# Loads of u, v and z kept apart from DMA block turns, outputs moved to the turns' queue, a third output buffer

## The chip, the cores and the metric

The kernel runs on one core of a Trainium2 chip. The metric is the device time of one execution in microseconds (us). Before the change three runs took 961.69, 960.47 and 951.78 us, median 960.47 us. A further execution was profiled; it took 950.05 us, and its span from first to last instruction is 948.3 us.

The engines' short names are those of the profile: PE (TensorE, matrix products), DVE (VectorE), ACT (ScalarE), POOL (GpSimd) and SP (SyncE). POOL and SP issue the DMA transfers here, each in the order of its own instruction stream; an instruction that waits holds back all that stands behind it in that stream.

## The reference

For each of 8 batches of 3072 rows, `u` and `v` have 256 columns, `z` has 64:

```python
scores = (1.0 / S) * np.matmul(z, z.transpose(0, 2, 1))
attn = np.maximum(scores, 0.0) ** 2
x = u * np.matmul(attn, v)                      # attention with a gate
g = np.maximum(x @ w1, x @ w2)                  # 1024 columns
out = g @ w_out                                 # 24576 x 256, float32
```

The scores of a batch are symmetric, so a block of `attn` right of the diagonal is also, transposed, a block left of it.

## The kernel before

**Tiles.** Rows come in tiles of 128 (24 in a batch), groups of 4 tiles (`G`, 6 in a batch), and couples of 2 groups (3 in a batch, named (b, c)). `attn` is kept in blocks of 4 x 4 tiles, `blk`, 128 partitions x 2048 bf16, 512 KB each; 27 slots (`NSLOTS`) are used in turn.

**Scores.** `score_pair` (line 190) makes two tiles' worth of a block: two matmuls from `zT` into PSUM (`s_ps`, four buffers), Relu by ACT into `r_sb` (line 217), the square by DVE into the block (lines 223, 225). Only blocks on and right of the diagonal are computed. A block right of the diagonal is turned by one DMA transpose into the slot of its mirror image (`mirror`, line 244, issued on SP). A diagonal block is computed as a triangle from batch 1 on, and three small DMA transposes fill the rest (line 228). A turn may be issued once its scores are there and its target slot is free.

**The first four groups** (batch 0, groups 0 to 3) run in a plain form (lines 619 to 699), with products at line 262. Some of their mirrors wait in the list `later` and are turned during groups 1 to 3.

**A couple** (loop at line 747, products at line 835). From batch 1 on, the product of a couple with `v` is made by seven products of half size in place of eight. Their operands are sums of blocks (S1, S3 ahead, S2, S4 during the couple; `combine`, line 297, DVE at line 300) and of pieces of `v` (`combine_v`, line 157: four differences, in the tile `vt`). Each product is worked by the two halves of PE's rows, at different times, in two lanes (`LANES`); where the halves of one product follow each other, the second waits for a `nop` on POOL that waits for the first (the relay, lines 844 to 849). The sums stand in four PSUM banks, `acc0` to `acc3`. Score pairs of later blocks are spread evenly over the couple's steps, so the turns come out evenly too, and the last scores of a couple are finished just after its last step.

**After a couple's last step** comes, in program order:

1. `loads_behind(i)` (line 704): loads of `u` for the next couple, and of pieces of `v` and `z` for the next batch, all issued on POOL;
2. DVE's work for the next couple: S1 and S3 of three block groups, at the first couple of a batch with `combine_v` of three pieces of `v` ahead of them (the first two differences of the piece loaded last stand fifth and sixth), and then the gates (line 415), which multiply by the turned `u` (`uT`);
3. `ff(i-1)` on PE (line 426): the gated unit and the output product of the couple before. It puts its four sums into the same banks `acc0` to `acc3` (`banks`, line 430). `leave` (line 471) copies each to SBUF on ACT (`o_sb`, line 475) and sends it to HBM (line 476): two half-way, two at the end.

Then the next couple begins. Its steps 2 and 6 issue the turns of `u` (`turn_u`, line 178, two buffers, freed by the gates of the couple before), step 8 or 30 the turn of a piece of `z` (`turn_z`, line 130), and then come the block turns. The recording is done under a manual schedule: each engine's instructions stand in the order in which they are written, and semaphores are set from the tiles that they read and write.

**Queues.** SP issues all turns (`mirror`, the triangles, `turn_u`, `turn_z`), and the four outputs of the last couple. POOL issues all loads and the other 92 outputs. A tile pool with n buffers lets its (n+1)th tile wait for the release of the first: `opool` has 2 buffers, so the third output copy waits until the first output has landed.

The names to follow: `load_z` 122, `turn_z` 130, `load_v` 142, `combine_v` 157, `load_u` 174, `turn_u` 178, `mirror` 244, `ff`/`leave` 426/471, `loads_behind` 704.

## Time and profile before

| What | Value |
|---|---|
| Runs | 951.78 to 961.69 us, median 960.47 |
| Profiled execution | 950.05 us, span 948.3 us |
| Busy time of DVE, ACT, POOL | 683.5, 633.6, 140.4 us |
| Mean granted PE clock | 0.984 |
| DMA packets | 146.01 MB, mean 154 GB/s |
| Read from HBM, written | 59.77 MB, 25.17 MB |
| Mirrors and triangle turns (`blk<-blk`) | 246, 4.7 us from issue to landing |
| Output on POOL (`out_dram<-o_sb`) | 92, 256 KB each, 4.2 us to landing |
| Output on SP | 4, 256 KB each, 2.1 us to landing |
| Load of `v` / `u` / `z` (most) | 84 / 48 / 21; 128 / 256 / 128 KB in SBUF; 8.4 / 7.2 / 8.4 us to landing |

How to read it. Busy time is a union of the times of an engine's instructions; a PE that is busy is not at its peak. A line of waits reads: the engine and what it waited to do, what released it, us in total, number of times, longest. A line of a timeline reads: start and duration in us, engine, line, operation, output and input tile, number of instructions, and in brackets the idle time before it and what ended it; `SPq` is SP's sequencer, and the time of a DMA there is the time that its issue took. The time from issue to landing counts from the start of the issue until the semaphore of the transfer has risen.

### The profile page before, as it was taken

The page shows a single profiled execution, that of the slowest core. Times are in us where ns is not written, and L with a number is a line of the kernel's source. Part 1 is how long each engine was busy: PE and PEld are TensorE (multiplying, and loading weights), DVE is VectorE, ACT ScalarE, POOL GpSimd, SP SyncE. Part 2 cuts the span into 40 slices and gives each one's busy share as a digit, 9 for nine tenths or more (in the row PEclk, how much of TensorE's full clock was granted, in tenths as well). Part 3 has the DMA queues.
Part 4 walks back from the last instruction along what each step waited for, and adds up shares of the span by engine and source line. Part 5 has one row for each costly group of instructions (what it writes and reads, how often), then busy time and mean ns, then how long its engine had stood idle before and what let it go on. Part 6 is the DMA issues. An engine that isn't in the chain of part 4 may idle for free.

```text
span 948.3 us, 19578 instructions
## 1 busy us (share of the span) xinstructions
PE 909.4 (96%) x7490; PEld 532.4 (56%) x7538; DVE 683.5 (72%) x1043; ACT 633.6 (67%) x1219; POOL 140.4 (15%) x266
## 2 busy tenths in 40 slices
PE   9994799999999999999989999999979999999998
PEld 4453355675655655655546656566445664655655
DVE  6770369696897689786786968968768687795542
ACT  6783587667676777767756677776746767674443
POOL 3121022020210210220202102102111021101000
PEclk9998799999999999999999999999999999999999
DMA  9999796999988988989989899799996987996401
GB/s 183 167 190 149 151 214 121 195 119 199 187 128 182 178 155 160 176 139 190 141 145 194 129 175 176 132 207 133 172 148 126 193 160 150 160 116 134 96 18 73
DMA packets 391838, 146.01 MB, mean 154 GB/s; under 512 B 362944, under 2 KB 377664, under 8 KB 391744
## 3 DMA queue, kind: packets, MB, share of 16 engines
q1 hardware_dynamic: 359904, 91.14, 61.9%
q0 software_dynamic: 31840, 53.62, 29.5%
q8 instruction: 59, 0.97, 0.4%
q14 instruction: 35, 0.29, 0.1%
HBM read 59.77 MB, written 25.17 MB: 90 GB/s over the span
## 4 chain that ended last, share of the span: by engine, by line
PE 85%; issue 4%; DMA 4%; SPq 2%; DVE 2%; POOL 1%; ACT 1%; ACTq 0%; DVEq 0%; POOLq 0%
PE acc L835 41%; PE acc L457 19%; PE d_ps L435 15%; PE s_ps L204 6%; PE acc L262 4%; DMA out_dram<-o_sb 3%; SPq L246 2%; DMA blk<-blk 1%; POOL v_sb L150 0%; DVE blk L300 0%; ACT r_sb L217 0%; DVE blk L225 0%; PE acc L597 0%; DVE blk L223 0%; ACT o_sb L475 0%
## 5 line engine op out<-in xcount | busy, mean ns | idle before, releaser
L217 ACT ACTIVATE r_sb<-s_ps 128x512 bf16<-128x512 f32 (+3 forms) x664 | 331.1, 559 | 113.4 <-PE s_ps L204 72.6
L835 PE MATMUL acc<-blk,vt 64*128 64x512 bf16 x2016 | 370.8, 379 | 9.9 <-ACT o_sb L475 9.9
L835 PE MATMUL acc<-blk,v_sb 64*128 64x512 bf16 x1704 | 345.8, 380 | 18.2 <-DMA blk<-blk 18.0
L300 DVE TENSOR_TENSOR blk<-blk,blk 128x2048 bf16<-128x2048 bf16 x252 | 302.0, 1221 | 23.2 <-PE acc L835 17.9
L448 ACT ACTIVATE g_sb<-d_ps 128x512 bf16<-128x512 f32 x376 | 217.9, 602 | 110.6 <-PE d_ps L435 89.9
L225 DVE TENSOR_TENSOR blk<-r_sb 128x1024 bf16<-128x1024 bf16 x251 | 170.5, 691 | 141.1 <-ACT r_sb L217 138.9
L457 PE MATMUL acc<-w_out_sb,g_sb 128*128 128x256 bf16 x1536 | 226.5, 273 | 0.0
L435 PE MATMUL d_ps<-xT,w_sb 128*128 128x512 bf16 x720 | 214.2, 379 | 2.6 <-issue 0.2
L835 PEld LDWEIGHTS <-vt 64*128 64x128 bf16 x2016 | 154.1, 95 | 92.8 <-issue 8.1
L835 PEld LDWEIGHTS <-v_sb 64*128 64x128 bf16 x1704 | 133.6, 95 | 119.0 <-DMA blk<-blk 18.3
L457 PEld LDWEIGHTS <-g_sb 128*128 128x128 bf16 x1536 | 150.3, 98 | 83.9
L204 PE MATMUL s_ps<-zT 64*128 64x512 bf16 (+3 forms) x672 | 148.6, 360 | 0.9 <-DVE r_sb L215 0.5
L476 POOL DMA_DIRECT2D out_dram<-o_sb x92 | 49.9, 547 | 381.8 <-ACT o_sb L475 366.9
L475 ACT COPY o_sb<-acc 128x512 f32<-128x512 f32 x96 | 52.1, 590 | 62.3 <-DMA out_dram<-o_sb 34.1
L435 PEld LDWEIGHTS <-w_sb 128*128 128x128 bf16 x768 | 73.3, 98 | 28.2 <-issue 9.8
L223 DVE TENSOR_TENSOR blk<-r_sb 128x512 bf16<-128x512 bf16 (+3 forms) x170 | 46.4, 320 | 40.0 <-ACT r_sb L217 39.8
L204 PEld LDWEIGHTS <-zT 64*128 64x128 bf16 x672 | 45.8, 95 | 47.9 <-issue 13.0
L150 POOL DMA_DIRECT2D v_sb<-in_v_dram x90 | 48.5, 566 | 148.3 <-PE acc L835 107.1
L771 DVE TENSOR_TENSOR h_sb<-h_sb,acc 128x512 f32<-128x512 f32 x84 | 55.4, 681 | 6.7 <-PE acc L835 6.7
L415 DVE SCALAR_TENSOR_TENSOR xT<-h_sb,uT 128x512 bf16<-128x512 f32 x96 | 59.9, 684 | 0.0
L176 POOL DMA_DIRECT2D un<-in_u_dram x48 | 26.2, 559 | 207.7 <-PE acc L835 161.5
L262 PE MATMUL acc<-blk,v_sb 64*128 64x512 bf16 x384 | 50.8, 376 | 1.7 <-DVE blk L225 1.1
(50 smaller groups left out, 274.8 us busy)
## 6 DMA issues: line engine op xcount, KB each, us to landing
out_dram<-o_sb POOLq DMA_DIRECT2D x92, 256.0 KB, 4.2
un<-in_u_dram POOLq DMA_DIRECT2D x48, 256.0 KB, 7.2
v_sb<-in_v_dram POOLq DMA_DIRECT2D x84, 128.0 KB, 8.4
blk<-blk SPq DMA_TRANSPOSE x246, 4.7
zn<-in_z_dram POOLq DMA_DIRECT2D x21, 128.0 KB, 8.4
v_sb<-in_v_dram POOLq DMA_DIRECT2D x6, 256.0 KB, 7.5
blk<-in_moe_w_dram POOLq DMA_DIRECT2D x2, 512.0 KB, 7.0
out_dram<-o_sb SPq DMA_DIRECT2D x4, 256.0 KB, 2.1
```

The source lines that it names most:

```text
L204: nc.tensor.matmul(s_ps[h][:, lo[h] :], zT[rows, z_at(b, blk * G + tiles[h]), :], zT[rows, q + lo[h] // P : q + G, :].rearrange("p t c -> ...
L217: nc.scalar.activation(o, s, AF.Relu)
L225: nc.vector.tensor_mul(a[:, k : k + 2, :], r, r)
L262: nc.tensor.matmul(a.out(acc[half, dc]), v_at(b, t, dc)[rows], a.moving(rows, j), start=first, stop=last,)
L300: op(*((by_key(x) if mixed else x.ap) for x in blocks))
L415: lambda dc=dc: nc.vector.scalar_tensor_tensor(out=x[:, dc, :].rearrange("p (t r) -> p t r", r=P), in0=hs[dc].rearrange("p (t r) -> p t r" ...
L435: nc.tensor.matmul(d_ps, w15_sb[:, kc, ts(nb, P)], xs[q][:, kc, :], start=(kc == 0), stop=(kc == KD - 1),)
L448: nc.scalar.activation(g_sb[q, nb], d_ps, AF.Relu)
L457: nc.tensor.matmul(o_ps[key][:, t % 2, :], x[:, ts(t, P)], w, start=first, stop=ends and t % 2 == 1 and n == len(weights) - 1,)
L475: nc.scalar.copy(o_sb, o_ps[q, h])
L771: nc.vector.tensor_add(out, a, b_)
L835: mm = nc.tensor.matmul(a.out(acc[name]), w()[rows], a.moving(rows, j), start=first, stop=left[name] == 0, skip_group_check=True,)
```

## The change

Four edits go together. (1) Two helpers, `turn` and `load`, wrap the DMA calls. A load marked `alone` waits until the last turn that was issued before it, in program order, has landed; the next turn or output behind a group of such loads waits until the last load of the group has landed. Only the first of several loads, and the first of several turns or outputs, carries the wait. All loads of `loads_behind` are marked so. (2) All outputs are issued on SP. (3) `opool` has three buffers. For that room, `vt` shrinks from four parts to three: the difference B22 - B12 overwrites B12 in the loaded piece of `v`, and P7 reads its weights there. (4) Two early loads in batch 0 (`z` piece 2 and `v` piece 2 of batch 1), which began during group 3 behind a small memset each, move into `loads_behind` of couple (0, 1), with `load_v(1, 1)`.

```diff
-    opool = ctx.enter_context(tc.tile_pool(name="opool", bufs=2))
+    opool = ctx.enter_context(tc.tile_pool(name="opool", bufs=3))
...
+    turned, loaded = [], []
+
+    def behind(go, others):
+        while others:
+            tc.add_manual_dep(go.ins, others.pop().ins.name, AFTER, reason="one at a time")
+
+    def turn(out, in_):
+        go = nc.sync.dma_start_transpose(out, in_)
+        behind(go, loaded)
+        turned[:] = [go]
+
+    def load(out, in_, alone=False):
+        go = nc.gpsimd.dma_start(out=out, in_=in_)
+        if alone:
+            behind(go, turned)
+            loaded[:] = [go]
...
-        nc.sync.dma_start_transpose(
+        turn(
...
-        t = tpool.tile([P, 4, G, P], bf16, name="vt")
+        t = tpool.tile([P, 3, G, P], bf16, name="vt")
...
-            lambda: nc.vector.tensor_sub(t[:, 2], b22, b12),
+            lambda: nc.vector.tensor_sub(b12, b22, b12),
             lambda: nc.vector.tensor_sub(t[:, 1], b22, t[:, 0]),
-            lambda: nc.vector.tensor_sub(t[:, 3], b21, t[:, 1]),
+            lambda: nc.vector.tensor_sub(t[:, 2], b21, t[:, 1]),
...
-        "P7": ("S3", 2),
+        "P7": ("S3", 12),
...
-        "X21": ("A22", 3),
+        "X21": ("A22", 2),
...
                 nc.scalar.copy(o_sb, o_ps[q, h])
-                (nc.sync if last else nc.gpsimd).dma_start(out=dst, in_=o_sb)
+                behind(nc.sync.dma_start(out=dst, in_=o_sb), loaded)
...
-                if (i, n) == (3, 14):
-                    load_z(1, 2, held=True)
-                if (i, n) == (3, 18):
-                    load_v(1, 2, held=True)
...
         def loads_behind(i):
             b, c = couples[i]
+            if (b, c) == (0, 1):
+                load_z(1, 2, alone=True)
             if c == 2 and b + 1 < B:
-                load_v(b + 1, 0)
+                load_v(b + 1, 0, alone=True)
             if i + 1 < len(couples):
                 for q in range(2):
-                    load_u(couples[i + 1][0], 2 * couples[i + 1][1] + q)
+                    load_u(couples[i + 1][0], 2 * couples[i + 1][1] + q, alone=True)
+            if (b, c) == (0, 1):
+                load_v(1, 2, alone=True)
+                load_v(1, 1, alone=True)
             if b and b + 1 < B and c < 2:
-                load_z(b + 1, c + 1)
-                load_v(b + 1, c + 1)
+                load_z(b + 1, c + 1, alone=True)
+                load_v(b + 1, c + 1, alone=True)
             if c == 2 and b + 2 < B:
-                load_z(b + 2, 0)
+                load_z(b + 2, 0, alone=True)
...
         loads_behind(PLAIN // 2 - 1)
-        load_v(1, 1)
```

More of the change, by code (lines that the diff above doesn't have):

```diff
@@ L120, in zT_pe, with load_z @@
         copy(zT[:, lo : lo + n, :], tp)
-    def load_z(b, piece, held=False):
+    def load_z(b, piece, held=False, alone=False):
         zn[b, piece] = zpool.tile([P, 2 * G, dqk], bf16, name="zn")
@@ L125, in load_z @@
             nc.vector.memset(zn[b, piece][:, 0, 0:1], 0.0)
-        nc.gpsimd.dma_start(
-            out=zn[b, piece], in_=by_tile(z[b])[:, ds(piece * 2 * G, 2 * G), :]
-        )
+        load(zn[b, piece], by_tile(z[b])[:, ds(piece * 2 * G, 2 * G), :], alone)
     def turn_z(b, piece):
@@ L140, with load_v @@
     vp, vt = {}, {}
-    def load_v(b, piece, lo=0, n=2 * G, held=False):
+    def load_v(b, piece, lo=0, n=2 * G, alone=False):
         if (b, piece) not in vp:
@@ L145, in load_v @@
         t = vp[b, piece]
-        if held:
-            nc.vector.memset(t[:, lo, 0:1], 0.0)
         step = 2 if b else n
         for at in range(lo, lo + n, step):
-            nc.gpsimd.dma_start(
-                out=t[:, ds(at, step), :], in_=by_tile(v[b])[:, ds(piece * 2 * G + at, step), :]
-            )
+            load(t[:, ds(at, step), :], by_tile(v[b])[:, ds(piece * 2 * G + at, step), :], alone)
     def v_at(b, t, dc):
@@ L164, in combine_v, with load_u @@
             lambda: nc.vector.tensor_sub(t[:, 0], b12, b11),
-            lambda: nc.vector.tensor_sub(t[:, 2], b22, b12),
+            lambda: nc.vector.tensor_sub(b12, b22, b12),
             lambda: nc.vector.tensor_sub(t[:, 1], b22, t[:, 0]),
-            lambda: nc.vector.tensor_sub(t[:, 3], b21, t[:, 1]),
+            lambda: nc.vector.tensor_sub(t[:, 2], b21, t[:, 1]),
         ]
     un, uT = {}, {}
-    def load_u(b, g):
+    def load_u(b, g, alone=False):
         un[b, g] = unat.tile([P, G, D], bf16, name="un")
-        nc.gpsimd.dma_start(out=un[b, g], in_=by_tile(u[b])[:, ds(g * G, G), :])
+        load(un[b, g], by_tile(u[b])[:, ds(g * G, G), :], alone)
     def turn_u(b, g):
         t = upool.tile([P, G, KD, P], bf16, name="uT")
-        nc.sync.dma_start_transpose(
+        turn(
             t.rearrange("p a c r -> p (a c) r"), un[b, g].rearrange("p a d -> p (a d)")
@@ L227, in finish @@
                 for j in range(G - 1):
-                    nc.sync.dma_start_transpose(
+                    turn(
                         a[:, j + 1 :, ts(j, P)], a[:, j, (j + 1) * P :]
@@ L245, in mirror @@
         t = Block(turned=True)
-        nc.sync.dma_start_transpose(
-            t.ap.rearrange("p (k r) -> p k r", r=P), A[b, g, blk].ap
-        )
+        turn(t.ap.rearrange("p (k r) -> p k r", r=P), A[b, g, blk].ap)
         A[b, blk, g] = t
```

## The prediction

> **What bounds the kernel now.** I read the busy shares first, then the waits of TensorE (PE), then the chain of waits inside one stall, and last the two DMA-issuing queues as a timeline.

> The page: PE is busy nearly everywhere, and so are the DMA engines, two thirds of that with block turns (q1), one third with loads and outputs (q0).

> ```profile
> PE 909.4 (96%) x7490; PEld 532.4 (56%) x7538; DVE 683.5 (72%) x1043; ACT 633.6 (67%) x1219; POOL 140.4 (15%) x266
> ...
> DMA  9999796999988988989989899799996987996401
> ...
> q1 hardware_dynamic: 359904, 91.14, 61.9%
> q0 software_dynamic: 31840, 53.62, 29.5%
> ```

> PE's idle time is 948.3 - 909.4 = 38.9 us, so no more can be won. The waits name its two large parts (us, times, longest), and one of SyncE's (SP's) that matters below:

> ```profile
> PE acc L835 <- DMA blk<-blk: 18.0, 1, 18.0
> PE acc L835 <- ACT o_sb L475: 9.9, 3, 5.7
> SPq L180 <- DVE xT L415: 61.6, 11, 10.4
> ```

> The chain of waits around the longest of the three `o_sb` stalls (start, us) shows its mechanism: an output lands, ScalarE (ACT) may overwrite that buffer, and only then has PE its bank back.

> ```profile
> 696.47 12.73 DMA out_dram<-o_sb
> ...
> 709.29 0.59 ACT o_sb L475
> ...
> 709.93 0.58 PE acc L835
> ```

> The granted clock, by stretch, tells the rest of a stall's price: it was 0.50 from 96 to 101 us, during the 18.0 us stall, and 0.71 from 710 to 716, after the 5.7 us one. A 6 us stretch at 0.71 loses 1.7 us; the 1.2 us stall has no such mark.

> Last the queues. SP behind the end of couple (1,2), T0 = 237.3 us, and GpSimd (POOL) at that end:

> ```profile
> 237.29 2.15 POOL L150 DMA_DIRECT2D v_sb<-in_v_dram  x4 [17.83 <-PE acc L835]
> 239.38 1.11 POOL L176 DMA_DIRECT2D un<-in_u_dram  x2
> 240.42 0.60 POOL L126 DMA_DIRECT2D zn<-in_z_dram  x1
> ```

> ```profile
> 256.99 2.66 SPq L180 DMA_TRANSPOSE uT<-un  x2
> 259.75 2.09 SPq L246 DMA_TRANSPOSE blk<-blk  x1
> 261.95 4.30 SPq L228 DMA_TRANSPOSE blk<-blk  x3
> 266.34 1.26 SPq L134 DMA_TRANSPOSE zT<-zd  x1
> 267.70 3.77 SPq L228 DMA_TRANSPOSE blk<-blk  x3
> 271.57 19.07 SPq L246 DMA_TRANSPOSE blk<-blk  x4
> ```

> SP works without a break from 257.0 on and still has four mirrors to issue when couple (2,0) ends at T0 = 272.2. They take 19 us because the loads run beside them. Alone, mirrors start 2.43 us apart (116.27, 118.78, 121.21, 123.60) and land 4.7 us after issue (page).

> **The change, part by part.** Let T0 be the end of a couple's steps. From the traces of PE, ACT and DVE behind 237.3: `ff` fills PE until T0+17.5 (254.81); the third and fourth `o_sb` copies come at T0+17.4 and 18.0; P5 needs the fourth copy's bank at T0+20.9 (258.2), and the third score pair, at T0+20.8 (258.06), needs ACT to have done the first.

> *Edits at nothing.* `vt` in three parts: `L165` takes 0.42 us wherever it writes, and weight loads from `vt` and `v_sb` both cost 95 ns; were the strided write twice as long, 0.4 us on DVE per piece. Two memsets go: POOL waits less, before anything needs it. 92 outputs leave POOL (0.54 us each) for SP, where four rows show 0.34 us: 1.4 us of SP per couple, in front of the `uT` turns; counted below.

> *Third buffer.* Now only the fourth copy waits for the first output's landing. This alone removes the three stalls: 9.9 us, and 1.7 us of slow clock behind the two larger ones, **-13.3 us**.

> *The wait of the loads.* They start when the last turn emitted has landed, not at T0. Seven loads (1.1 MB in SBUF): the last is issued 3.1 us after the first (240.42 - 237.29), and the least crowded z load landed in 3.4 us: at least 6.5. With bandwidth: at the start of the kernel 256 KB loads land 1.28 us apart (v issued 2.46, landing 6.4 later; the sixth after it issued 5.64, landing 10.9 later), so 4.5 x 1.28 plus 2.9 for the first bytes (3.6 us for the v load at 127.0, less its own 0.64) = 8.7 at most. I take D = 7.6.

> What stands behind the first waiting load on POOL: the other loads, and then the next couple's relay `nop`s (line 844), through which one half of PE's work waits for the other. P1 ends in lane 0 at T0+20.7 and its other half starts six steps of 0.22 us later, at T0+22.1. With the last turn at T0+14.1 (below) the loads are issued by T0+17.8: covered, by some 3 us; a turn that lands later than that makes PE wait for the relay.

> *The wait of the outputs.* The next item in SP's queue after the loads is the first output, so it waits for their landing, LL; behind it stand three outputs, two `uT` and the whole next train. Output lands 2.3 us later (2.1 on the page from SP), copy 0.6, two relus 1.1: PE's stall is S = LL + 4.0 - 20.8, that is **S = (LL - T0) - 16.8**. The other end counts P5's bank alone: S = (LL - T0) - 18.0.

> Now the three kinds of boundary.

> Behind c=2. The last mirrors wait for their scores, in before too: 346.55 is issued 1.3 us before T0 = 347.8, and two follow. Alone: 346.55 + 2 x 2.43 + 4.7 = T0+8.3; I take 7.5, since SP may be ahead. The fourth v load lands 5.3 us later, T0+12.8 (it was 8.4), and LL = T0+15.1: no output stall. But `combine_v` of this piece stands first on DVE, with 10 us of `vt` and `blk` work behind it: it ended at 255.7, and PE takes the last S3 at 258.5, so slack 2.8. Stall 12.8 - 8.4 - 2.8 = 1.6 (1.3 to 3.4). The gates behind move by 4.4, and SP's `uT` waits for them (the third line of waits): from T0+19.7 to 24.1.

> Behind c=0. The train from 256.99 to its landing, alone, is 271.57 + 3 x 2.43 + 4.7 - 256.99 = 26.6. So the last turn lands 24.1 + 26.6 = 50.7 after the old T0; the couple ends at 34.95 + 1.6 = 36.55: T0+14.1. LL = T0+21.7, **S = 4.9**, plus 1.7 of clock.

> Behind c=1. `uT` follow the fourth output, LL + 3.4 from the previous boundary; two uT, zT, three mirrors and twelve triangle turns at 1.28 land 28.9 later. The couple ends 36.5 + 6.6 after the previous T0. With LL = 21.7: 21.7 + 3.4 + 28.9 - 43.1 = T0+10.9, LL = T0+18.5, **S = 1.7**, and half of the clock's 1.7.

> Sum: batches 1 to 6, 6 x (6.6 + 2.6) = 55; seven boundaries behind c=2, 7 x 1.6 = 11; batch 7 loads only u, none. **+66 us.**

> *The stall at 83 us.* It ends with a mirror that loads held up (two mirrors issued at 66.27 and 71.12 took until 86.2). Alone, six more turns are issued by 77.3 and land at 82. But now eleven loads (10.5 us) follow, to 92.5, then `turn_z`, then the outputs: 96.2, copy, PE starts at 97 and not 101. The slow clock starts as early and then covers more work: I take **-2**; if turns and loads were both gone from this place, -18 - 2.5.

> From the profiled 950.05 us (span 948.3): 950.05 - 13.3 + 66 - 2 = **1000**. The profiled execution lies at the low end of the runs (median 960.47); I add nothing, because part of that spread may be the very `o_sb` stalls that go. With the cheap ends (D = 6.5, bank alone) S is 2.6 and about 0.6, sum +38: 973; with the dear ones (D = 8.7, c=2 stall 3.4) +90: 1025.

> [...]

> **The rivals.**
> 1. *The turns are done in time, and the kernel is faster* (12%). If LL comes by T0+16.8 behind c=0 and c=1, no output is late. For it: without loads beside them the trains end earlier than before, and source-bound turns may not queue up. Against it: SP is already unbroken from `uT` to the couple's end, and it starts no earlier. Price: 950.05 - 13.3 - 2 = 935, or 917 if the first stall goes too.
> 2. *A draw* (7%): output stalls of about 1 us at twelve boundaries and 0.5 us at seven, +15, cancel the gain: 950 to 970 with the runs' spread. A difference of 1% is about what this kernel's measurement can tell.
> 3. *Late turns hold up more than outputs* (8%). Turns 5 us later reach the S sums (`L300`; it waits for turns only 3.0 us now) and scores that reuse blocks, or the loads are issued after T0+20.7 and PE waits for POOL's relays. 2 us more at 20 boundaries: 1040.
> 4. The forecast (73%): 973 to 1025.

> Slower by over 1%: 81%. The range 956 to 1030 leaves out most of rivals 1 and 3.

> **What would show it.** Right: PE waits for `ACT o_sb` some 12 times or more, 2 to 6 us each, behind c=0 and c=1; POOL's loads wait for `DMA blk<-blk`; SP's output waits for a load; mirrors never take over 3 us to issue; the clock row dips all through. Wrong: PE's idle time below 30 us, or loads that land within 5 us of their first issue.

## The result, and the profile after

The changed kernel took 1062.70 us, median of 4 runs (1061.53 to 1069.21); the kernel before took 956.12 us beside it (4 runs, 951.24 to 961.69). The ratio is 1.113, 95% interval 1.104 to 1.122: slower by 11%. The prediction said slower, with 1000 us and a range up to 1030, so the direction held and the size did not: from the profiled 950.05 us it added 50, and the profiled execution after (1069.21 us, span 1067.3 us) adds 119. Some executions of a kernel are over 1.5% longer than its fastest; the medians here include them and the ratios do not, so a ratio need not be the quotient of two medians.

The page of the changed kernel, the busy shares, clock, DMA and queue lines that were shown of the kernel before:

```profile
PE 957.7 (90%) x7490; PEld 552.9 (52%) x7538; DVE 682.0 (64%) x1041; ACT 632.4 (59%) x1219; POOL 90.6 (8%) x174
...
PEclk9996989898999998989999989898899998999999
DMA  9998867868677696766968678686786867858212
...
q1 hardware_dynamic: 373152, 115.26, 54.9%
q0 software_dynamic: 24480, 29.50, 18.3%
```

The loss is in two parts. PE's idle time is 1067.3 - 957.7 = 109.6 us, up by 70.7. PE's busy time rose by 957.7 - 909.4 = 48.3 us for the same 7490 matmuls: the clock row now dips all through, and the mean granted clock fell from 0.984 to 0.942. The DMA row, 9 nearly everywhere before, is now mostly 6 to 8.

What the change was for did happen: 17 of the 246 block turns took over 3 us to issue, the longest 9.2, where 66 had before, the longest 15.0. The prediction's sign said that none would.

The waits of the changed kernel (us in total, times, longest):

```profile
POOL un L76 <- DMA blk<-blk: 207.7, 5, 43.6
...
PE acc L844 <- ACT o_sb L484: 62.0, 13, 19.3
DVE vt L175 <- DMA v_sb<-in_v_dram: 56.7, 7, 9.2
...
PE acc L844 <- DVE blk L309: 26.3, 17, 3.2
```

The stalls on output copies grew from 9.9 us in 3 to 62.0 us in 13: the six couple ends behind c=0, the six behind c=1, and the first couple's stall of 19.3 us, which before was put down to a mirror and lasted 18.0. The seven waits of DVE for `v`, and PE's for the S sums (`blk L309`), are the ends behind c=2. POOL's loads wait for turns and the clock dips, as written under what would show the prediction right.

The chain of waits behind couple (1,1) of the changed kernel (start, us) shows one output stall from end to end. The last turn had landed at 228.59.

```profile
229.14 0.86 POOL un L76 x2
...
232.26 6.70 DMA v_sb<-in_v_dram
238.96 0.02 SPq L485
...
239.01 2.02 DMA out_dram<-o_sb
...
241.13 0.59 ACT o_sb L484
...
241.76 0.61 PE acc L844 x2
```

The seventh load lands 9.8 us after the first was issued (238.96 - 229.14), within 0.05 us SP issues the first output, 2.0 us later it has landed, and only then may the fourth copy take its buffer. PE stood idle from 237.47 to 241.76. It is exactly the predicted chain; its first link is longer than was allowed for.

Then the clock, by stretch around that stall (us, PE busy and matmuls, the other engines, granted clock, DMA share, GB/s):

```profile
237.50:241.10 3.60, 0.00 (x0) 0.00 (x0) 0.00 (x0) 0.00 (x0) 0.00 (x0) 1.00 0.39 136
241.10:248.00 6.90, 6.24 (x29) 2.44 (x30) 2.75 (x6) 4.62 (x9) 0.00 (x0) 0.51 0.91 211
248.00:251.00 3.00, 3.00 (x32) 1.50 (x29) 3.00 (x4) 2.26 (x5) 0.00 (x0) 1.00 0.86 162
```

The 4.29 us of waiting are followed by 6.9 us at half clock: 29 matmuls in 6.24 us, where the next 3 us hold 32. That is another 3.1 us (6.24 x 0.49), or 3.5 us if it is reckoned by matmuls (6.24 - 29 x 3.0 / 32). Over the whole trace PE was busy for 91.8 us at half clock, before for 11.9 (busy time inside the stretches that the traces record at half clock). Half of the difference is 40 us, so slow clock accounts for most of the 48.3 us.

How the couples' stretches changed, each from the first product of `ff` behind its last step to the same point of the next couple (us, summed from the two traces):

| Stretch | Before | After | Difference | Predicted |
|---|---|---|---|---|
| first (0,1) | 61.4 | 63.6 | +2.2 | -2 |
| six behind c=0 | 218.8 | 249.1 | +30.4 | +39.6 |
| six behind c=1 | 223.4 | 269.6 | +46.2 | +15.3 |
| seven behind c=2 | 272.9 | 313.6 | +40.7 | +11.2 - 13.3 |

The three stalls of before lie in the last row, so the gain of the third buffer is counted there.

### The profile page after: what moved, and what is told of

Same layout as the page of the kernel before. It is cut to its first block, busy times and chain, and to the rows that moved or that the text cites. A ratio compares the mean times of both kernels' runs of the same rounds, so it can differ in the third digit from the quotient of the medians.

```text
span 1067.3 us, 19596 instructions
## 1 busy us (share of the span) xinstructions
PE 957.7 (90%) x7490; PEld 552.9 (52%) x7538; DVE 682.0 (64%) x1041; ACT 632.4 (59%) x1219; POOL 90.6 (8%) x174
## 2 busy tenths in 40 slices
DMA packets 397727, 146.01 MB, mean 137 GB/s; under 512 B 362945, under 2 KB 377665, under 8 KB 397633
## 3 DMA queue, kind: packets, MB, share of 16 engines
q1 hardware_dynamic: 373152, 115.26, 54.9%
q0 software_dynamic: 24480, 29.50, 18.3%
## 4 chain that ended last, share of the span: by engine, by line
PE 57%; DMA 20%; DVE 11%; issue 5%; POOL 4%; ACT 2%; SPq 0%; ACTq 0%; DVEq 0%; POOLq 0%
PE acc L844 31%; DMA v_sb<-in_v_dram 10%; PE acc L466 9%; PE d_ps L444 9%; DVE blk L309 6%; PE s_ps L215 5%; DMA blk<-blk 4%; DMA out_dram<-o_sb 3%; PE acc L271 3%; POOL v_sb L76 3%; DMA zn<-in_z_dram 1%; DVE blk L236 1%; DMA un<-in_u_dram 1%; POOL un L76 1%; DVE xT L424 1%
## 5 line engine op out<-in xcount | busy, mean ns | idle before, releaser
L844 PE MATMUL acc<-blk,v_sb 64*128 64x512 bf16 x2208 | 437.7, 398 | 54.0 <-DVE blk L309 26.3
L228 ACT ACTIVATE r_sb<-s_ps 128x512 bf16<-128x512 f32 (+3 forms) x664 | 329.8, 562 | 147.4 <-PE s_ps L215 64.9
L844 PE MATMUL acc<-blk,vt 64*128 64x512 bf16 x1512 | 346.9, 403 | 42.6 <-ACT o_sb L484 42.6
L309 DVE TENSOR_TENSOR blk<-blk,blk 128x2048 bf16<-128x2048 bf16 x252 | 301.6, 1219 | 33.8 <-PE acc L844 31.5
L844 PEld LDWEIGHTS <-v_sb 64*128 64x128 bf16 x2208 | 169.8, 98 | 224.1 <-issue 106.9
L215 PE MATMUL s_ps<-zT 64*128 64x512 bf16 (+3 forms) x672 | 187.1, 376 | 2.0 <-DVE r_sb L226 0.5
L844 PEld LDWEIGHTS <-vt 64*128 64x128 bf16 x1512 | 132.3, 99 | 91.1 <-issue 25.2
L215 PEld LDWEIGHTS <-zT 64*128 64x128 bf16 x672 | 58.7, 98 | 42.1 <-issue 11.2
L76 POOL DMA_DIRECT2D v_sb<-in_v_dram x90 | 48.3, 567 | 274.9 <-PE d_ps L444 194.2
L271 PE MATMUL acc<-blk,v_sb 64*128 64x512 bf16 x384 | 50.4, 376 | 2.3 <-DVE blk L236 1.1
L466 PE MATMUL acc<-W2o_sb,xT 128*128 128x256 bf16 x384 | 49.9, 273 | 0.7 <-DVE h_sb L290 0.7
```

Source lines behind the costliest of these rows:

```text
L76: go = nc.gpsimd.dma_start(out=out, in_=in_)
L215: nc.tensor.matmul(s_ps[h][:, lo[h] :], zT[rows, z_at(b, blk * G + tiles[h]), :], zT[rows, q + lo[h] // P : q + G, :].rearrange("p t c -> ...
L228: nc.scalar.activation(o, s, AF.Relu)
L271: nc.tensor.matmul(a.out(acc[half, dc]), v_at(b, t, dc)[rows], a.moving(rows, j), start=first, stop=last,)
L309: op(*((by_key(x) if mixed else x.ap) for x in blocks))
L466: nc.tensor.matmul(o_ps[key][:, t % 2, :], x[:, ts(t, P)], w, start=first, stop=ends and t % 2 == 1 and n == len(weights) - 1,)
```

## The experiments

The theory after the result: every wait of the change makes its own chain late, by the loads' landing and by the last turn's, and the chains hide each other; at each couple end the latest shows. The rivals: moving the outputs to SP's queue costs it (no wait needed), or whatever waits, the time in which loads have the DMA engines to themselves is lost.

The first six kernels take away the waits, or what makes a late output cost, in steps. All are the changed kernel with the edit shown.

**Outputs free of the loads**

```diff
-                behind(nc.sync.dma_start(out=dst, in_=o_sb), loaded)
+                nc.sync.dma_start(out=dst, in_=o_sb)
```

> The changed kernel, but no output waits for loads (loads still wait for the last turn, and the next turn for the loads). My theory: behind c=0 and c=1 PE stalls because the fourth output copy waits for the first output, and that one for the loads; these stalls (7 and 5 us long with their slow clock, some 75 us in all) go, those behind c=2, where VectorE waits for v, stay: 985 to 1000 us, and PE waits for the output copies under 10 us in all. Rival, the move of the outputs to SP's queue is what costs, because they stand behind turns there: 1050 us or more.

Measured: 1034.79 us, neither number. Behind c=0 the stalls are gone wholly (36.4 us a stretch, as in the kernel before). Behind c=2 the late `v` stays. Behind c=1 a new stall of 4.7 to 8.0 us begins 27 us after the couple's end. Its wait, and the chain at the one that ends at 241.87:

```profile
PE s_ps L215 <- DMA zT<-zd: 38.7, 6, 8.0
```

```profile
224.94 7.37 DMA zn<-in_z_dram
...
238.58 3.25 DMA zT<-zd
241.87 0.61 PE s_ps L215
```

This is a chain that the prediction's sum did not have: the next batch's `z` is loaded behind c=1, turned by `turn_z`, and needed by its first scores in the same couple. The load waits for the last turn, and then the turn of `z`, behind the two of `u`, waits for the last load. In the changed kernel, where no such wait shows, the output stall comes earlier in the couple and pushes these scores back.

**The `v` loads of c=2 at once**

```diff
-                load_v(b + 1, 0, alone=True)
+                load_v(b + 1, 0)
```

> The changed kernel, but the four loads of v behind c=2 do not wait for the last turn (u and z still do). My theory: the stalls behind c=2 come from the fourth v load, which now lands 15 to 17 us after the couple's end and has 10 us of VectorE work behind it; landing 7 to 9 us after the end it costs nothing, and 40 to 55 us of 55 go: 1005 to 1025 us. Rival, the outputs' wait is the cause behind c=2 as well: 1050 us or more.

Measured: 1039.79 us, 23 us less than the changed kernel and 15 more than the upper end of the expectation. The fourth `v` load now lands 6.4 to 7.0 us after the first product of `ff` behind a c=2 end (13.5 to 15.7 before this edit) and PE no longer waits for S sums. But the `u` and `z` loads still wait, and the output stalls, now 20, take the place:

```profile
PE acc L844 <- ACT o_sb L484: 82.7, 20, 17.7
```

**A fourth output buffer**, all waits kept (the room is taken from the gate products)

```diff
-    gpool = ctx.enter_context(tc.tile_pool(name="gpool", bufs=8))
-    opool = ctx.enter_context(tc.tile_pool(name="opool", bufs=3))
+    gpool = ctx.enter_context(tc.tile_pool(name="gpool", bufs=7))
+    opool = ctx.enter_context(tc.tile_pool(name="opool", bufs=4))
```

> The changed kernel with a fourth output buffer (and one of the eight buffers of the gate products given up to make room); all waits stay. Theory (behind the first and second couples PE waits because the fourth output copy needs the buffer of the first output, whose transfer is held until the loads have landed): no PE stall on output copies behind the first and second couples of the iterations, the v stall behind the third couples as in the changed kernel, the z turn stall of 4.7 to 8.0 us behind the second couples as where outputs are free; the time is within 10 us of 1034.8, the kernel with outputs that do not wait. Rival (the held outputs also crowd the turns behind them, buffers or not): 1050 us or more.

Measured: 1036.35 us, 1.6 us from the kernel with free outputs. The outputs are as late as in the changed kernel (issued 17 to 20 us after the first product of `ff` at c=0 ends), yet no fourth copy waits for one: behind c=0, where a stretch takes 36.4 us again, buffer reuse was the whole price of late outputs. Behind c=1 it is not. The `z` turn appears again, as expected, but its six stalls are 51.9 us in all, where outputs do not wait 38.7: the late outputs stand ahead of the turns of `u` and `z` in SP's queue, and the first `uT` is issued 1.9 us after the last load's landing instead of 0.1. So the near equal times are partly chance: the six stretches behind c=1 are 11 us longer, the others 9 us shorter. In the first couple the cover of POOL's relays, some 3 us in the prediction, broke: a relay stands behind the late loads there. In the couple after it PE waits 13.7 us for the S sums. The waits of PE in this kernel:

```profile
PE s_ps L215 <- DMA zT<-zd: 51.9, 6, 9.4
PE acc L844 <- DVE blk L309: 28.5, 16, 13.7
PE acc L844 <- DVE h_sb L780: 11.5, 7, 1.6
PE acc L844 <- POOLq L853: 5.1, 2, 4.8
...
PE acc L844 <- ACT o_sb L484: 0.6, 1, 0.6
```

**Outputs free and `v` at once**, both edits above (not the buffer)

> The changed kernel with two of its waits gone: outputs do not wait for loads, and the v loads behind the third couple of an iteration go out at once. The turns still wait for the loads, so the z turn behind the second couple stays late. Theory (three separate late chains, each hidden by the next): behind the first couples and the third couples no stall above 1 us and about 36.4 to 38 us a couple; behind the second couples the PE stall on the z turn of 4.7 to 8.0 us stays. Without outputs: 1034.8 less some 6 x 6.5 = 995 us (985 to 1005). Rival (what costs is the time in which the loads hold the DMA engines, whatever waits for it): another stall takes the place of the v stall behind the third couples and the time stays above 1020 us.

Measured: 991.79 us, as the theory has it. Behind c=0 and c=2 no stall above 1 us is left; the six `z` stalls of 6.5 to 8.4 us stay.

**And the turns free**, with the two edits before it: of the waits only that of the loads for the last turn is left

```diff
         go = nc.sync.dma_start_transpose(out, in_)
-        behind(go, loaded)
         turned[:] = [go]
```

> As the kernel before it in this group, and the turns do not wait for the loads either: the only wait left is that of the loads for the last block turn. Theory (the wait of the turns for the loads is what makes the z turn late behind the second couples): its landing comes 3 to 5 us earlier, the stall there falls from 4.7 to 8.0 us to 0 to 3 us, and the time is 960 to 980 us. Rival (the late loads are enough by themselves, as z lands 8 us after the last turn and the turns then run beside loads at 5 to 15 us each): the stall stays at 5 us or more, and the time is within 8 us of the kernel with both waits.

Measured: 964.48 us, in the theory's range. The `z` stall falls to 2.2 to 5.2 us, more than the 0 to 3 expected. SP behind couple (1,1), in the kernel where turns wait and then in this one (the couple ends are 0.3 us apart):

```profile
212.53 5.38 SPq L485 DMA_DIRECT2D out_dram<-o_sb  x4
226.75 2.62 SPq L71 DMA_TRANSPOSE uT<-un  x2
229.45 1.29 SPq L71 DMA_TRANSPOSE zT<-zd  x1
```

```profile
210.17 7.38 SPq L484 DMA_DIRECT2D out_dram<-o_sb  x4
217.65 7.42 SPq L71 DMA_TRANSPOSE uT<-un  x2
225.16 1.26 SPq L71 DMA_TRANSPOSE zT<-zd  x1
```

The `uT` turns start 9.1 us earlier and need 4.8 us more to be issued among the loads. So the rival is partly right as well: here a turn beside loads is dearer, but it is still 4.3 us earlier than one that waits for them.

**No wait at all** (the outputs stay in SP's queue, with three buffers)

```diff
     def load(out, in_, alone=False):
         go = nc.gpsimd.dma_start(out=out, in_=in_)
-        if alone:
-            behind(go, turned)
-            loaded[:] = [go]
```

> The changed kernel without any wait between loads and turns or outputs: outputs on SP, three buffers, loads as early as their buffers allow. My theory: the waits are the cost, so this comes back to 945 to 985 us; what may remain is outputs that stand on SP behind turns which take 5 to 15 us to issue beside loads. Rival, the move to SP is the cost: above 1030 us.

Measured: 945.13 us (the kernel before beside it: median 953.59), then in a second measurement:

> The changed kernel without any of its waits (outputs in the queue of the turns, three output buffers, three places for the combined v, the loads of the third piece of z and v of the second iteration moved behind the first couple), timed in five rounds. Theory: the waits are the whole loss, and the moved loads shorten the first couple's stretch by 3 to 5 us: 0.990 to 0.998 of the kernel before. Rival: one look at 945.1 us was a fast draw, and the ratio is 1.00 or above, as the outputs behind the block turns cost PE 0.3 to 1.7 us at some couples.

940.27 us, ratio 0.987, interval 0.982 to 0.993: slightly better than the theory's range. The waits are the whole loss, and the rest of the change is a gain of some 1.3%. The staircase, in us: 1062.7 with all waits, 1034.8 with outputs free, 991.8 with `v` at once besides, 964.5 with turns free besides, 940.3 with loads free too. Only the first and last values are medians of several runs. Every step is over 20 us, but 13 executions of the kernel before, beside these, lay between 936.96 and 962.92 us, so a step from one run to another is known only roughly; that each step takes a wait of PE away is read from the traces. `v` at once saves 23 us alone and 43 where the outputs are free: the chains hide each other. Both rivals fall: with the outputs still on SP nothing is lost, and with two waits gone the loads still wait for the turns, yet the time is 991.8 us, not above 1020.

The next kernels ask which part brings the gain.

**Buffer and `vt` alone** (the kernel before with three output buffers and the overwritten piece of `v`; outputs on POOL, loads where they were)

```diff
-    opool = ctx.enter_context(tc.tile_pool(name="opool", bufs=2))
+    opool = ctx.enter_context(tc.tile_pool(name="opool", bufs=3))
...
```

> The kernel before with the third output buffer and the difference of v made in place, outputs still on POOL. My theory: the three output stalls of 1 to 6 us and their slow clock go, 10 to 15 us less than before, ratio 0.985 to 0.99. Rival, the in-place difference (VectorE writes the piece of v that PE reads) costs: no gain, or slower than before.

Measured: 948.45 us, ratio 0.997, interval 0.989 to 1.005: no gain that can be told. The wait of PE for the output copies did not go; there are now five, of the fourth copy for the first output:

```profile
PE acc L835 <- ACT o_sb L475: 7.2, 5, 2.5
```

**The moved loads alone** (the kernel before; `z` and `v` piece 2 and `v` piece 1 of batch 1 go out behind the first couple, without a wait)

```diff
-                if (i, n) == (3, 14):
-                    load_z(1, 2, held=True)
-                if (i, n) == (3, 18):
-                    load_v(1, 2, held=True)
...
             b, c = couples[i]
+            if (b, c) == (0, 1):
+                load_z(1, 2)
...
+            if (b, c) == (0, 1):
+                load_v(1, 2)
+                load_v(1, 1)
...
-        load_v(1, 1)
```

> The kernel before with one part of the change alone: the loads of the third piece of z and v and of the second piece of v of the second iteration go out behind the first couple, without a wait; two output buffers, four places for the combined v, outputs in the queue of the loads. Theory (these moved loads are what the kernels without waits gain): the first couple's stretch falls from 61.4 to 54 to 57 us, and the time is 0.985 to 0.995 of the kernel before. Rival (the gain of 1.3 to 1.5% needs the third output buffer): 0.996 to 1.003.

Measured: 949.95 us, ratio 0.993, interval 0.988 to 0.998. The first stretch is 56.4 us where it was 61.4, as in the kernel without waits, so the moved loads do shorten it by 5.0 us. That the whole kernel gains is not settled: the ratio says 0.7%, the medians (951.65 us for the kernel before beside it) 0.2%. How the 1.3% is shared among the parts is not shown.

**No waits, outputs on POOL** (with the edit of the kernel without waits)

```diff
-                behind(nc.sync.dma_start(out=dst, in_=o_sb), loaded)
+                (nc.sync if last else nc.gpsimd).dma_start(out=dst, in_=o_sb)
```

> As the one before it, but with the outputs back in the queue of the loads, as in the kernel before. Theory: the outputs are issued 10 and 17 us after the loads are released instead of 10 to 20 us, PE does not wait for them except behind the third couples, and the time is 0.985 to 0.995 of the kernel before, 1 to 4 us under the kernel with outputs in the queue of the turns. Rival: the loads of eight pieces behind the third couple delay the outputs by 1 to 3 us each time, which eats what the queue of the turns cost: the two are within 2 us of each other.

Measured: 939.84 us, ratio 0.985, interval 0.979 to 0.992, within 0.5 us of the one on SP. The queue of the outputs makes no difference that can be told.

**The same two with a fourth output buffer** (the edit of the four-buffer kernel above)

> No waits between loads, turns and outputs, outputs in the queue of the loads, the moved loads, and four output buffers (seven of the eight gate buffers). Theory (the 8.5 us that PE still waits for output copies with three buffers come from the fourth copy, which a fourth buffer frees): PE's waits for output copies fall below 1 us in all, and the time is 0.975 to 0.985 of the kernel before. Rival (the late outputs then hold up the next item, or the missing gate buffer makes the products of the gated unit wait): 0.985 or above.

> The same with the outputs in the queue of the turns, as the change has it. Theory: PE's waits for output copies, 3.9 us with three buffers, fall below 1 us, 0.978 to 0.987 of the kernel before, and within 4 us of the kernel with outputs in the queue of the loads. Rival: 0.987 or above, as the missing gate buffer costs what the output buffer brings.

Measured: 932.55 us, ratio 0.988 (0.983 to 0.992), and 934.85 us, ratio 0.989 (0.986 to 0.993). The waits for output copies are gone, as expected; the largest wait of PE in the second is the first couple's, which comes of the scores there:

```profile
PE d_ps L441 <- ACT r_sb L225: 10.8, 1, 10.8
...
PE acc L841 <- ACT o_sb L481: 0.6, 1, 0.6
```

Both ratios lie on the rivals' side of what was written, and overlap with those of three buffers. So four versions without waits beat the kernel before by 1.1 to 1.5%, and the fourth buffer adds nothing that these runs can tell.

## Why the prediction was wrong in size

The mechanism was the predicted one, link by link: POOL's loads wait for the turns, SP's first output for the loads, the fourth copy for that output, PE for the copy; behind c=2 DVE's `combine_v` for `v`. Rivals 1 and 2 (no stall, a draw) did not happen. What failed are sizes, and two of them make nearly the whole error: the slow clock behind each stall, put at 11.9 us and measured at 48.3, and the landing of the loads, which with the waits behind it makes the idle time 70.7 us in place of 38.9. T0 is taken 1.8 us ahead of the first product of `ff`, as in the trace before (237.29 and 239.06); measured values are means over the six or seven couple ends.

| Term | Predicted | Measured |
|---|---|---|
| Last turn lands behind c=0 / c=1 / c=2 | T0 + 14.1 / 10.9 / 7.5 | T0 + 10.3 / 12.2 / 9.2 |
| That landing to the first load's issue | 0 | 0.6 |
| D, seven loads behind c=0 / c=1 | 7.6, at most 8.7 | 9.4 / 9.8 |
| First load to the fourth `v` (c=2) | 5.3 | 6.7 |
| S = (LL - T0) less | 16.8, or 18.0 (bank alone) | 17.9 |
| PE idle per end, c=0 / c=1 / c=2 | 4.9 / 1.7 / 1.6 | 2.4 / 4.7 / 4.9 |
| Busy time added per end (slow clock), c=0 / c=1 / c=2 | 1.7 / 0.85 / 0 | 2.5 / 3.0 / 2.3 |
| PE busy time, net | +11.9 (15.3 - 3.4) | +48.3 |

**The formulas held; the loads did not.** With the measured inputs and 18.0 the sum gives 10.3 + 0.6 + 9.4 - 18.0 = 2.3 behind c=0, 12.2 + 0.6 + 9.8 - 18.0 = 4.6 behind c=1 and 9.2 + 0.6 + 6.7 - 8.4 - 2.8 = 5.3 behind c=2, against 2.4, 4.7 and 4.9 measured. D was wrong beyond its stated upper end. That end took 1.28 us per 256 KB from the start of the kernel; behind (1,1) the 3.5 such pieces after the first landed in 238.96 - 233.35 = 5.6 us, 1.6 us each. The lower end took a `z` load that had landed in 3.4 us, but the last of seven lands 6.7 us after its own issue. Why the pace is 1.6 and not 1.28 is not shown here.

**The turns took the time that the sum gave them; the couples did not.** From the first `uT` to the last landing the trains took 27.5 us where 26.6 was predicted (landing behind c=0) and 30.1 where 28.9 was (c=1). Behind c=1 the last turn landed 53.7 us after the previous T0, predicted 54.0 (two errors of over 1 us cancel: `uT` began at 23.6 and not at 25.1). Behind c=0 it landed at 55.5, predicted 50.7, because `uT` began at 28.0 and not at 24.1: the gates waited longer for `v`. But the couple ahead of it, with its own stall and its slow clock, took 45.1 us and not 36.55, so this later landing came only 10.3 us after its end. So the stall behind c=0 is half of the predicted one: the couple before had already lost the time.

**The clock is the largest miss.** The idle time was predicted at +38.9 net (50.8 less the 9.9 and 2) and measured at +70.7; the busy time at +11.9 and measured at +48.3. So 36 of the 69 us that were missing are busy time, most of it at half clock. The step said "1.7 us" behind c=0, half of it behind c=1, none behind c=2. The 1.7 came from the 5.7 us stall of the kernel before, and the same view at finer cuts shows what that number was:

```profile
706.60:709.90 3.30, 0.00 (x0) 0.00 (x0) 0.00 (x0) 0.61 (x2) 0.00 (x0) 0.51 1.16 168
709.90:713.50 3.60, 3.57 (x18) 1.53 (x19) 1.38 (x2) 2.44 (x5) 1.07 (x2) 0.50 0.59 189
```

The half clock lasted 6.9 us there too, but half of it lay inside the stall, where it costs nothing. After the 4.29 us stall shown above nearly all of it lies behind. So the stall of 4.29 us made more slow work (3.1 us) than the one of 5.7 (3.57 x 0.50 = 1.8), and the row by itself did not say so; after which stalls half clock came stands in the last section. For the same reason "no more can be won" than the idle 38.9 us was not right: of the busy time before, 11.9 us ran at half clock.

**The third buffer, -13.3.** In the changed kernel no output stall is left behind c=2, where the three had been, but there DVE's wait for `v` took their place, so none of the gain is seen. Tried alone the step was too large: 7.2 us of output stalls in five places stayed, since the fourth copy then waits for a first output that is late behind the loads.

**The first stall, -2**, became +1.3 us of idle time (19.3 for 18.0) and +2.2 in the stretch: the eleven loads behind it landed at 98.5, not 92.5, and were issued from 85.2 on, when the last turn had landed at 84.7, not 82.

**Edits at nothing** held. The kernels without waits carry the smaller `vt`, its overwritten operand and SP's 92 more issues, and are faster than before.

**Rival 3**, late turns that hold up more than outputs, is real, but hidden in the changed kernel: the `z` turn comes out once the outputs are free, and POOL's relay once there is a fourth buffer.

**Whether keeping loads and turns apart brings bandwidth** is not shown: the two queues' packets took (61.9% + 29.5%) of 948.3 = 867 us of the engines' time before and (54.9% + 18.3%) of 1067.3 = 781 us after, for the same 146.01 MB, but the times of packets overlap (from 272 to 293 us of the kernel before they come to 1.15 of the engines' time), so these sums are not the time for which the engines were busy.

## What to carry to other kernels

A transfer that is made to wait for another's landing adds the whole latency of both to whatever stands behind it in both queues: behind couple (1,1), 9.8 us from the first load's issue to the last one's landing, and 2.0 us more for the output. So before adding such a wait, follow every consumer to its first use, not only the one that is late now; where several chains are close, removing one shows the next (`v` at once saved 23 us alone and 43 where the outputs were free). Price a stall of PE at its length plus the slowed work behind it, here 2.3 to 3.0 us for each couple end. Late outputs cost through the reuse of their buffers, which one more buffer takes away (PE's waits for output copies went from 62.0 us to 0.6), and through the turns that stand behind them in the queue, which it does not (the `z` stalls there were 51.9 us).

## What the runs showed of the hardware

```profile
326.48:329.89 3.41, 1.56 (x11) 0.47 (x8) 0.00 (x0) 1.59 (x4) 0.00 (x0) 1.00 0.67 248
329.89:333.30 3.41, 3.37 (x18) 2.26 (x19) 2.30 (x6) 2.11 (x6) 0.00 (x0) 0.50 0.98 212
```

- So the length of a stall alone did not tell. In the kernel where only loads wait, a stall of 2.89 us ending at 228.53 put 2.08 us of idle PE into one piece and 0.81 into the next, and two pieces of half clock followed; one of 2.94 us ending at 344.92 was cut into 1.80 and 1.14, and none did:

```profile
224.31:227.73 3.42, 1.34 (x14) 0.39 (x8) 3.42 (x4) 1.74 (x4) 0.00 (x0) 1.00 1.02 199
227.73:231.14 3.41, 2.60 (x14) 0.94 (x16) 1.95 (x3) 1.08 (x2) 0.00 (x0) 0.50 1.10 206
231.14:234.55 3.41, 3.41 (x20) 1.19 (x18) 3.03 (x4) 1.08 (x2) 0.00 (x0) 0.50 1.15 214
...
340.37:343.78 3.41, 1.61 (x16) 0.52 (x12) 3.41 (x4) 2.01 (x4) 0.00 (x0) 1.00 1.25 188
343.78:347.19 3.41, 2.27 (x22) 1.09 (x24) 2.66 (x4) 1.42 (x3) 0.00 (x0) 1.00 1.12 196
```

- *Loads kept apart from turns went with less packet time.* The 867 us before and 781 us in the changed kernel stand beside (58.8% + 20.3%) of 989.8 = 783 us with the outputs free and `v` at once, and (62.9% + 21.3%) of 962.5 = 810 us with the turns free besides. Of these four kernels the one with the least packet time was the slowest.
